# Linear attention and a channel mix on one Trainium2 core: q of batch 4's first group turned by the DMA crossbar, with a new order of all instructions

## The chip, the cores and the metric

The kernel runs on one core of one Trainium2 chip. The metric is the device time of one execution in microseconds, lower is better. Times of several runs are given by their median; one further execution was taken with the hardware profiler, and all rows below are from it.

## The reference

Eight batches, eight heads, 576 positions, head width 64. The output of the attention goes, with the heads side by side (512 channels), into a channel mix.

```
def _attn_ref(q, k, v):                       # (8, 8, 576, 64) each
    q_s = exp(q - max(q, -1)); q_s = q_s / sum(q_s, -1)
    k_s = exp(k - max(k,  2)); k_s = k_s / sum(k_s,  2)
    kv = einsum('bhsd,bhse->bhde', k_s, v)
    return einsum('bhsd,bhde->bhse', q_s, kv)

def _moe_ref(x, mu_k, mu_r, w_k, w_v, w_r):   # x (8, 576, 512), w_k to 1024 and w_v back
    x_prev = x shifted by one position, zero first
    xk = mu_k * x + (1 - mu_k) * x_prev
    xr = mu_r * x + (1 - mu_r) * x_prev
    v = max(xk @ w_k, 0) ** 2 @ w_v
    return v / (1 + exp(-(xr @ w_r)))
```

## The kernel before, in words

**Groups.** The attention is done in 16 groups (b, g): batch b, and of it four heads, two on each half of the partitions and two beside each other (`load`, L190). For each group q, k and v are loaded as f32; ACT takes the exponentials of q and k (`exp`, L326) and casts v (`cast_v`, L332); DVE sums q's exponentials, takes reciprocals and scales q (`rsum`, `rrec`, `scale_q`, L341 to L353). TensorE (PE) forms K-V products and the sums of k (`kv`, L389), and for batch 0 the sums apart (`zs`, L380).

**Turning q.** The product of q with K-V needs q with its width on the partitions. There are two ways. In the first, PE transposes the scaled q, 64 rows at a time, against an identity into PSUM (`transpose_q`, L362: 18 or 36 matmuls) and ACT copies the result to the tile qt (`copy_qt`, L371). In the second, for the groups in the tuple CROSSBAR (L40), SP issues a DMA that transposes from the tile qs to the tile qt (L516), and neither PE nor ACT has a part in it. Such a DMA makes 1,152 packets of 256 bytes in the trace.

**Blocks.** From batch 2 on, PE's work for a group is one block, named B with batch and group (L447): the X product of the group before it, which the list `pending` holds over (`x`, L532); the transposes of q, unless the crossbar does them; and K-V. B40 is the block of (4, 0) and holds X of (3, 1); B41 holds X of (4, 0). The first groups have T (transposes), KV and Z (sums) or, in batch 1, a TKV block, and X products of their own, in which the mix's weights are already folded (`mixed_x`, L480). After X, ACT and DVE copy, shift and mix x into the rings xk and xr.

**Units.** The mix works through ten units of up to 512 positions. In a name such as k37, r21, v230, the first digit is the unit: k is a block of 128 columns of the product with w_k (`k_part`, L618, four matmuls; in units 0 and 1 the first four blocks come in two parts), r one with w_r (`r_part`, L650, four), v one with half of w_v (`v_part`, L670, four). Units 4 and 9 have 256 positions. ACT applies ReLU and tanh, DVE squares and gates, and SP stores in halves of 128 KB from the seven th buffers (L682).

**The order.** Nothing is scheduled by a tool. The string ORDER (L43) lists every operation by name, and for those that take buffers their numbers after a colon; each engine gets its instructions in this order. Within one engine, a waiting instruction holds all behind it. POOL issues nearly all loads (eleven raw buffers), and each of its DMAs waits for the landing of the one eight places before it. SP issues the first loads, all stores and the crossbar's transposes. `fill` (L292) are matmuls of zeros at the start that write a bank of PSUM.

Of the kernel before, what the change touches and what calls it, by code (L numbers as in the profile page):

```python
# [51 lines left out]
X001:0.3 kvn01:1 wp010:1 k02:0 x0010 edge01 k00:1 x0011 X010:1.0 load11q1 k03:2 x0100 x0101 k01:3
wv0 rsum100:2 k00.2 expk100:2 load10v1:7 k02.2 wp011 expq110:0 k03.2 relu00:0 k01.2 load10v0
X011:0.1 relu01:1 k07:1 sq01:0 load11v0:8 sq00 expq101 k05:3 load11v1 relu02:2 rsum101 relu03:1
k06:0 rrec100 sq02 relu05:0 sq03 x0110 k04:2 x0111 relu06:2 sq05 load11k1:9 r00:3 relu07:1
load11k0 expk101 r02:0 expq111 wv1 r03:1 relu04:0 rsum111:3 th00:0 r01:2 sq07 th03:1 sq04 rrec101
th02:2 scale101:2 v020:3 wv2 scale100 cast101:0 v030:1 load20v0:10 rrec111 cast100 scale111:0
muload v000:0 th01:3 rsum110 cast110:1 v010:2 load20q0:0 rrec110 cast111 scale110 TKV10:0
expk111:0 load21q0:2 expk110 load30q0:1 rz10:2 kvn10:0 TKV11:1 qt10:2 wp100:0 load20k0:3 v011
load21v0:4 rz11:0 sq06 v031 kvn11:1 edge10 qt11:0 v021 wp110:1 load61v0:6 v001 v032 edge11 v002  # L60
cast200:2 X100:0.1 load21k0:5 o00 v022 load31q0:7 x1001 x1000 v012 o02 expq200:1 wp111 mu:0
X110:1.0 mucopy k13:3 load30v0:8 x1101 x1100 k11:0 wp101 o01 expq210:2 k13.2 rsum200:0 k11.2
load31k0:9 relu13:1 X111:0.1 relu11:0 load40q0:10 k12:2 x1111 x1110 k17:3 o03 expk200:1 load30k0:0
sq11:1 k10:0 st03.2 sq13 k16:1 st00 expq300:0 rrec200 rsum210:1 load40v0:2 st03 X101:1.0 st01
relu17:2 k12.2 x1011 st00.2 x1010 k10.2 load31v0:3 sq17 relu16:0 k14:3 scale200:1 relu10:1
relu12:2 r12:1 cast210:0 sq10 load60q0:1 TKV20:0 rsum300:2 relu14:1 r11:0 th12:4 rrec210 rrec300
load41q0:4 rz20:1 expk210:2 k15:2 sq12 w20:0 scale210:2 r10:3 qt20:1 v120:1 sq16 relu15:2
scale300:0 expq310:1 B21:1.0 load50q0:5 sq14 th10:5 v110:2 rz21:2 sq15 xs20:0 xb20 w21:1
load40k0:7 rsum310:3 v100:3 qt21:0 v121 edge20 diff20:0 th11:6 v111 cast300:1 sc2000:0 X21:0.1
sc2011:1 o11 r13:0 xs21:1 load41k0:8 xb21 sc2010 o12 v101 expk300:0 edge21 rrec310 r20:2 diff21:1  # L70
expk310:1 load41v0:0 sc2001 v130:1 sc2101:2 mix200 th20:1 load60v0:9 TKV30:1 sc2100 th13:0
sc2111:0 mix210 v131 cast310:2 sc2110 k27:2 cast400:0 o13 load51q0:3 rz30:0 k21:0 scale310:1
st13.2 relu27:0 load50k0:2 st13 expq400:2 k22:1 o10 k20:2 w30:2 relu22:1 load71v0:10 st10 mix201
qt30:2 st11 k23:3 sq27:0 st11.2 rsum400:0 relu21:2 k24:1 st01.2 relu23:0 st10.2 B31:0.1 mix211
expk400:2 sq23 k26:0 rz31:1 relu24:0 rrec400 load50v0:7 sq21 xb30:0 w31:0 k25:3 sq24 scale400:2
relu20:2 r22:1 xs30 qt31:1 sq20 r23:2 edge30 diff30:0 relu25:0 B40:1.0 relu26:2 sq22 sc3001:2
expq410:0 v200:3 sc3000 mix300 th22:0 v220:0 load71k0:4 rz40:2 sq25 th23:6 rsum410:1 xs31:1 r21:1
xb31 v230:2 sq26 expq500:1 edge31 sc3011:1 v201 diff31:1 cast410:1 load61q0:5 w40:1 v231 sc3101:0
sc3100 th21:3 rrec410 load61k0:0 mix310 v221 expq510:2 o23 r30:1 o20 qt40:0 load71q0:3 k33:2
scale410:0 st20.2 th30:5 st20 k37:3 relu33:1 st12.2 o22 k40:1 st12 relu37:0 sc3111:2 v210:2 sc3010  # L80
st02 expk410:0 rsum500:2 st02.2 k41:0 k35:3 expq600:0 load51k0:8 mix301 v211 sc3110 relu40:2
load51v0:1 sq37:1 k32:1 relu35:0 o21 expk500:1 sq33 B41:0.1 mix311 relu41:1 load70q0:2 sq35 k31:3
rz41:0 sq40:0 relu32:0 w41:2 sq41 k30:2 sq32 relu31:2 rsum510:3 cast500:2 k34:0 r31:1 relu30:1
rsum600:0 load70v0:7 relu34:0 r33:3 th31:1 sq30 xs40:0 rrec510 k36:2 xb40 rrec500 sq31 sq34 k44:0
scale500:1 relu36:1 r32:1 relu44:2 k43:2 edge40 qt50:1 th32:4 diff40:0 v330:0 qt41:2 sq36 v310:1
rrec600 st23.2 sc4001:0 th33:2 scale510:2 v331 expq610:1 k46:3 sc4000 qt51:0 relu43:0 o33
load60k0:5 B50:1.0 relu46:1 cast510:0 scale600:0 k47:2 st23 k42:0 cast600:1 v300:3 load70k0:1 sq46
qt60:2 sq44 rz50:1 mix400 v311 relu47:1 xs41:1 xb41 v320:2 o31 relu42:2 sq47 v301 expq700:2 st31.2
edge41 sq42 diff41:1 st21 r41:1 st21.2 expk510:2 o30 v321 sc4101:1 st30.2 sc4100 sq43 st31 k45:0
sc4110:2 mix410 st30 r40:3 relu45:1 expk600:0 o32 v410:0 sq45 rsum610:1 th41:6 k50:2 sc4111 k52:1  # L90
relu50:2 w50:0 rsum700:2 cast610:2 v411 k51:2 relu52:0 o41 mix411 k53:1 relu51:1 rrec610 B51:0.1
sq51:1 sq50 k54:0 scale610:1 xb50:1 v400:2 relu53:1 sc4010:0 relu54:2 rz51:2 sq52 k55:1 expq710:0
sc4011 rrec700 mix401 v401 relu55:0 rsum710:3 k56:0 th40:3 expk610:1 k57:1 sq53 sq54 relu56:1 sq55
r50:3 w51:1 relu57:2 scale700:2 r51:0 th50:1 cast700:0 v500:1 rrec710 o40 sq56 v510:3 th51:5 st40
sq57 xs50 st41 edge50 B60:1.0 st33 diff50:1 v501 st32.2 xb51:0 sc5000:1 st41.2 rz60:0 sc5001 v511
xs51 st40.2 w60:2 expk700:2 mix500 qt61:1 r52:2 o50 expk710:0 o51 B61:0.1 st50 edge51 v520:0
st50.2 sc5010:2 diff51:0 th52:6 st22 r53:1 cast710:1 st51 sc5011 sc5100:0 st51.2 sc5101 v521
sc5110:1 th53:3 mix510 v530:3 sc5111 rz61:1 mix511 k60:2 o52 xb60:0 v531 w61:0 st52 mix501
relu60:0 st32 k61:1 scale710:0 xs60 st52.2 B70:1.0 st22.2 relu61:1 o53 k62:0 xb61:1 sq60:0 st53
edge60 k63:2 relu62:2 st53.2 diff60:1 xs61 st33.2 k64:1 sq61 relu63:0 qt70:0 sc6000:0 sc6001 k65:3  # L100
sc6010:1 relu64:1 mix600 k66:0 sq62 edge61 relu65:2 sq63 k67:2 diff61:0 relu66:0 r60:1 sq64
sc6100:2 relu67:1 sc6101 r61:3 sq65 th60:1 mix610 v600:0 sq66 th61:5 sc6011 sq67 v610:2 sc6110:0
sc6111 mix601 v601 mix611 v611 rz70:2 w70:1 r62:1 o60 o61 st60 r63:3 th62:4 st60.2 v620:0 st61
th63:6 st61.2 v630:2 v621 v631 o62 k70:1 st62 o63 st62.2 k71:3 relu70:2 st63 st63.2 k72:0 sq70:1
relu71:0 qt71:2 k73:2 sq71 relu72:1 k74:1 sq72 relu73:2 k75:3 sq73 relu74:0 k76:0 sq74 relu75:1
k77:2 sq75 relu76:2 r70:1 sq76 relu77:0 B71:0.1 sq77 th70:0 v700:3 xb70:0 rz71:0 w71:2 r71:0 v701
th71:3 xs70 v710:2 o70 edge70 X71:1.0 st70 diff70:1 v711 xb71:1 st70.2 sc7000:2 r72:1 sc7001 xs71
o71 r73:0 edge71 st71 th72:2 mix700 st71.2 v720:3 diff71:0 th73:1 sc7010:1 v730:2 sc7100:0 sc7101
sc7110:2 v721 mix710 sc7111 v731 sc7011 o72 k80:1 mix711 st72 k81:0 st72.2 o73 relu80:1 mix701
st73 k82:3 relu81:2 st73.2 sq80:0 k83:2 sq81 relu82:0 k84:1 sq82 relu83:1 k85:0 sq83 relu84:2  # L110
k86:3 sq84 relu85:0 k87:2 sq85 relu86:1 r80:1 sq86 relu87:2 r81:0 sq87 th80:5 v800:3 th81:4 v810:2
v801 v811 o80 r82:1 st80 o81 st80.2 r83:0 th82:6 st81 st81.2 v820:3 th83:0 v830:2 v821 v831 o82
k90:1 st82 o83 k91:0 st82.2 relu90:0 k92:3 st83 relu91:1 sq90:1 k93:2 relu92:2 sq91 st83.2 k94:1
relu93:0 sq92 k95:0 relu94:1 sq93 k96:3 relu95:2 sq94 k97:2 relu96:0 sq95 r90:1 relu97:1 sq96 sq97
r91:0 th90:3 v900:3 th91:2 v901 v910:2 o90 v911 st90.2 st90 v910.2:1 o91 v911.2 st91.2 st91 o91.2
# [722 lines left out]
```

## Time and profile before

| | before |
|---|---|
| runs, median of 3 (lowest to highest) | 196.73 us (196.01 to 197.06) |
| profiled execution, its own time | 196.33 us |
| its span | 194.6 us |
| busy: PE, DVE, ACT, POOL | 186.5, 150.0, 140.7, 43.5 us |
| TensorE's granted clock, mean | 0.997 |
| DMA | 41.86 MB, mean 215 GB/s |

The span runs from the first to the last instruction of the program; the execution's own time has some 1.8 us around it. Rows of a timeline give start, length, engine, line, operation, out<-in with sizes, and in square brackets the idle time of that engine ahead of it and what ended it. Line numbers are those of the kernel before; in the changed kernel every line behind ORDER is one lower. A matmul of 128x512 starts 0.216 us after the one before it when PE is dense; its row is longer since matmuls are pipelined.

### The profile page before, as it was taken

The numbers are of one execution on the slowest core, as the hardware profiler recorded it, in microseconds if no ns is written. First come the engines' busy times: TensorE is split into PE (matmuls) and PEld (weight loads), VectorE is DVE, ScalarE is ACT, GpSimd is POOL, SyncE is SP. The second block draws the span as 40 slices with busy tenths as digits, with TensorE's granted clock in tenths as the row PEclk, the third lists the DMA queues.
The fourth block names the chain that finished last, engine by engine and source line by source line (L and its number), as shares of the span: only waits on it lengthen the run. The fifth ranks groups of instructions, "written<-read, shape, count | busy, mean of one in ns | idle before, by whom it ended". The sixth has DMA issues, their size and how long they took to land.

```text
span 194.6 us, 4767 instructions
## 1 busy us (share of the span) xinstructions
PE 186.5 (96%) x1873; PEld 90.6 (47%) x1873; DVE 150.0 (77%) x347; ACT 140.7 (72%) x218; POOL 43.5 (22%) x70
## 2 busy tenths in 40 slices
PE   7789999999999999999999999999999999999991
PEld 2254445445444554554555444444444444444751
DVE  1788658799999999999989998999924469622531
ACT  3678799899999999989996798767225742752440
POOL 8444348694324212341110000000000000000000
PEclk9999999999999999999999999999999999999998
DMA  6999999999999999899699604887049122404413
GB/s 200 316 261 291 267 351 302 397 394 393 414 390 394 394 407 334 280 333 320 171 212 125 220 0 100 172 190 154 0 110 138 34 54 54 111 0 95 94 29 108
DMA packets 23646, 41.86 MB, mean 215 GB/s; under 512 B 9404, under 2 KB 12744, under 8 KB 23624
## 3 DMA queue, kind: packets, MB, share of 16 engines
...
q14 instruction: 8, 0.07, 0.1%
HBM read 33.56 MB, written 9.44 MB: 221 GB/s over the span
## 4 chain that ended last, share of the span: by engine, by line
PE 81%; DMA 12%; POOL 3%; ACT 2%; issue 0%; DVE 0%; POOLq 0%
PE mm_c L672 11%; PE mm_d L672 9%; PE mm_c L620 8%; PE mm_a L620 7%; PE mm_b L620 7%; DMA wk_bb<-in_moe_w_k_dram 7%; PE mm_b L652 7%; PE mm_d L620 7%; PE mm_a L672 6%; DMA raw_h<-in_v_dram 5%; PE mm_b L672 5%; PE mm_a L652 4%; PE mm_d L652 3%; PE mm_c L652 1%; PE att_b L396 1%; PE att_a L536 1%
## 5 line engine op out<-in xcount | busy, mean ns | idle before, releaser
L672 PEld LDWEIGHTS <-k_a 128*128 128x128 bf16 x144 | 13.8, 98 | 16.4 <-issue 0.2
L652 PEld LDWEIGHTS <-xr 128*128 128x128 bf16 x144 | 13.9, 98 | 16.1 <-issue 0.2
L672 PEld LDWEIGHTS <-k_b 128*128 128x128 bf16 x152 | 14.4, 98 | 15.0 <-issue 0.2
L652 PE MATMUL mm_b<-wr,xr 128*128 128x512 bf16 x64 | 16.4, 379 | 0.0
L620 PEld LDWEIGHTS <-wk_ab 128*128 128x128 bf16 x80 | 7.6, 98 | 8.2 <-issue 0.8
L620 PEld LDWEIGHTS <-wk_bb 128*128 128x128 bf16 x80 | 7.8, 98 | 7.7
L620 PEld LDWEIGHTS <-wk_aa 128*128 128x128 bf16 x80 | 7.4, 98 | 8.2 <-issue 0.9
L620 PEld LDWEIGHTS <-wk_ba 128*128 128x128 bf16 x80 | 7.5, 98 | 7.8 <-issue 0.2
L652 PE MATMUL mm_a<-wr,xr 128*128 128x512 bf16 x36 | 9.3, 380 | 0.0
L672 PE MATMUL mm_c<-wv_a,k_a 128*128 128x512 bf16 x32 | 8.2, 379 | 0.0
L607 ACT ACTIVATE rel_b<-mm_b 128x512 bf16<-128x512 f32 (+1 forms) x7 | 4.0, 570 | 4.9 <-PE mm_b L620 4.8
L607 ACT ACTIVATE rel_a<-mm_b 128x512 bf16<-128x512 f32 (+1 forms) x8 | 4.6, 573 | 4.0 <-PE mm_b L620 3.6
L620 PE MATMUL mm_c<-xk,wk_aa 128*128 128x512 bf16 (+1 forms) x26 | 7.3, 363 | 0.0
L620 PE MATMUL mm_c<-xk,wk_ab 128*128 128x512 bf16 (+1 forms) x26 | 7.3, 363 | 0.0
L611 DVE TENSOR_TENSOR k_a<-rel_b 128x512 bf16<-128x512 bf16 (+1 forms) x14 | 5.4, 383 | 2.5 <-ACT rel_b L607 2.5
L672 PE MATMUL mm_d<-wv_a,k_b 128*128 128x512 bf16 x28 | 7.2, 379 | 0.0
L652 PE MATMUL mm_d<-wr,xr 128*128 128x512 bf16 x28 | 7.2, 379 | 0.0
L611 DVE TENSOR_TENSOR k_b<-rel_a 128x512 bf16<-128x512 bf16 (+1 forms) x14 | 5.5, 391 | 1.8 <-ACT rel_a L607 1.3
L607 ACT ACTIVATE rel_c<-mm_a 128x512 bf16<-128x512 f32 (+1 forms) x11 | 6.0, 550 | 0.7 <-PE mm_a L620 0.7
L611 DVE TENSOR_TENSOR k_b<-rel_b 128x512 bf16<-128x512 bf16 (+1 forms) x14 | 5.5, 391 | 1.3 <-ACT rel_b L607 0.9
L611 DVE TENSOR_TENSOR k_b<-rel_c 128x512 bf16<-128x512 bf16 (+1 forms) x12 | 4.7, 392 | 1.9 <-ACT rel_c L607 1.6
L620 PE MATMUL mm_d<-xk,wk_ba 128*128 128x512 bf16 (+1 forms) x22 | 6.1, 360 | 0.0
...
## 6 DMA issues: line engine op xcount, KB each, us to landing
...
```

What stands on the lines that cost most here:

```text
L396: kn.nc.tensor.matmul(kn.half(slot, r)[two[u], KVO:KVO + n], lhsT=kn.eks[ek.index][two[r], j, u, :], rhs=by, start=(j == 0), stop=(j == J ...
L536: kn.nc.tensor.matmul(kn.half(slot, u)[two[r], to:to + n], lhsT=kn.ws[w.index][two[u], r, :], rhs=x_columns(r, u, at, n), start=True, stop ...
L607: kn.nc.scalar.activation(out=kn.rels[rel.index][:, 0:n], in_=kn.bank(kf)[:, 0:n], func=ACT.Relu, scale=HALF_ROOT)
L611: kn.nc.vector.tensor_tensor(out=kn.k2s[k2.index][:, fc, 0:n], in0=kn.rels[rel.index][:, 0:n], in1=kn.rels[rel.index][:, 0:n], op=ALU.mult)
L620: kn.nc.tensor.matmul(kn.bank(kf)[:, 0:n], lhsT=kn.wk[fc // 4][ct % 2][:, ct // 2, (fc % 4) * 128: (fc % 4) * 128 + 128], rhs=kn.xs[0][:, ...
L652: kn.nc.tensor.matmul(kn.bank(rps), lhsT=kn.xs[1][:, ct, c:c + 128], rhs=kn.wr[:, ct, :], start=(ct == 0), stop=(ct == CT - 1))
L672: kn.nc.tensor.matmul(kn.bank(vps)[:, 0:width], lhsT=kn.k2s[k2.index][:, ft, 128 * m:128 * m + 128], rhs=wv_of(ft)[:, part], start=(ft == ...
```

## The change

The tuple of the groups whose q the crossbar turns gets a seventh member, (4, 0). Its 36 transposes and ACT's copy are gone with it, and SP issues a transposing DMA for it (qt40). ORDER is replaced as a whole: the same operations, permuted, with other buffer numbers. Cut to what the text speaks of:

```diff
-CROSSBAR = tuple((b, g) for b in range(5, B) for g in range(2))
+CROSSBAR = ((4, 0),) + tuple((b, g) for b in range(5, B) for g in range(2))
...
 ORDER = """
...
-load00k1 load01v late load01k0:3 load10q0:4 wk00 wk01 expq001:0 expq000 load11q0:5 rsum001:0
...
+load00k1 load10q0:3 load01k0:4 load01v wk00 load10q1 expq001:0 expq000 wk10 rsum001:0 rsum000 wk01
+expk000:0 rrec001 ACT!load01k1 wk11 rrec000 scale001:0 expq011:1 fill:1 fill.2:2 fill.3:3 fill.4:0
...
-widecopy wk10 rrec010 fill.17:1 KV001:0 rrec011 scale010:1 KV000 fill.18:2 fill.19:3 T00:1 rest
-Z00 qt00:0 scale011 rz00:0 expk010:1 fill.20:1 fill.21:1 T01:3 edge00 kvn00:0 load10q1 expk011
-fill.22:1 KV010:2 wp000:0 expq100:2 wr wp001 X000:1.0 qt01:1 KV011 x0001 Z01 load10k1 x0000 rz01:1
+rrec010 fill.17:1 fill.18:2 KV001:0 scale010:1 KV000 T00:1 rest Z00 qt00:0 rz00:0 scale011
+load11q0 expk010:1 kvn00:0 fill.19:3 fill.20:1 fill.21:1 T01:3 edge00 wp000:0 expk011 wp001
+X000:2.1 expq100:2 load10k0:6 qt01:1 fill.22:2 KV010:0 x0001 KV011 Z01 wr x0000 X001:1.3 rz01:1
...
+relu21:0 st12.2 B31:1.0 relu22:1 mix201 relu23:2 sq22 k24:3 cast400:0 rz31:1 rrec400 w31:0 mix211
+k26:0 relu20:1 load70v0:3 sq21 xs30:0 scale400:2 xb30 r22:1 r23:2 relu24:0 edge30 qt40:0 sq20
+qt31:1 sq24 k25:3 diff30:0 th22:4 B40:0.1 sq23 relu26:1 sc3001:0 r21:1 sc3000 relu25:0 rz40:2
...
```

In the order built from it, PE has 36 transposes fewer, ACT one copy fewer and SP one transposing DMA more; POOL's loads are the same set in another order. In the first stretch POOL now queues q of (1, 0) ahead of v of (0, 1), and w_k's tile wk10 ahead of wk01. On ACT the first half of k of (0, 0) goes ahead of q of (0, 1). On PE the transposes T00 follow KV000 directly, and the last zero matmul, fill.22, writes the third of the mm banks, one of the two that the transposes of (0, 1) have filled.

More of the change, by code (lines that the diff above doesn't have):

```diff
@@ L44 @@
 ACT!load00q0:0 zero ident load00q1 ACT!load00k0:1 load01q1:2 ACT!load01q0 rows load00v consts warm
-load00k1 load01v late load01k0:3 load10q0:4 wk00 wk01 expq001:0 expq000 load11q0:5 rsum001:0
-ACT!load01k1 rsum000 load10k0:6 expq011:1 rrec001 wk11 rrec000 rsum011:1 fill:1 fill.2:2 fill.3:3
-fill.4:0 fill.5:1 fill.6:2 fill.7:3 fill.8:0 fill.9:1 fill.10:2 fill.11:3 fill.12:0 fill.13:1
-fill.14:2 fill.15:3 fill.16:0 wide:0 scale000:0 expq010 expk000:0 rsum010 expk001 scale001
-widecopy wk10 rrec010 fill.17:1 KV001:0 rrec011 scale010:1 KV000 fill.18:2 fill.19:3 T00:1 rest
@@ L50 @@
-Z00 qt00:0 scale011 rz00:0 expk010:1 fill.20:1 fill.21:1 T01:3 edge00 kvn00:0 load10q1 expk011
-fill.22:1 KV010:2 wp000:0 expq100:2 wr wp001 X000:1.0 qt01:1 KV011 x0001 Z01 load10k1 x0000 rz01:1
[L52 to L115, printed above, removed]
@@ L116 @@
-st91.4 st91.3
+load00k1 load10q0:3 load01k0:4 load01v wk00 load10q1 expq001:0 expq000 wk10 rsum001:0 rsum000 wk01
+expk000:0 rrec001 ACT!load01k1 wk11 rrec000 scale001:0 expq011:1 fill:1 fill.2:2 fill.3:3 fill.4:0
+fill.5:1 fill.6:2 fill.7:3 fill.8:0 fill.9:1 fill.10:2 fill.11:3 fill.12:0 fill.13:1 fill.14:2
+fill.15:3 fill.16:0 wide:0 scale000 expq010 rsum011:1 rsum010 expk001 rrec011 widecopy load11q1:5
+rrec010 fill.17:1 fill.18:2 KV001:0 scale010:1 KV000 T00:1 rest Z00 qt00:0 rz00:0 scale011
@@ new lines @@
+load11q0 expk010:1 kvn00:0 fill.19:3 fill.20:1 fill.21:1 T01:3 edge00 wp000:0 expk011 wp001
+X000:2.1 expq100:2 load10k0:6 qt01:1 fill.22:2 KV010:0 x0001 KV011 Z01 wr x0000 X001:1.3 rz01:1
+kvn01:1 edge01 k02:0 wp010:1 x0010 k00:1 x0011 load10k1 X010:0.1 k03:2 x0100 x0101 k01:3 wv0
+expq101 wp011 rsum101:2 k02.2 load10v0:7 k00.2 relu02:0 rrec101 rsum100 k03.2 relu00:1 X011:0.1
+load10v1 relu03:2 sq00:0 k01.2 x0110 load11v1:8 sq03 k07:0 relu01:1 load11v0 expq111:0 k06:1 sq01
+load11k1:9 x0111 expq110 k05:2 scale101:2 relu07:2 rrec100 k04:3 sq07 relu05:1 sq02 relu06:2
@@ new lines @@
+rsum111:3 r03:0 load11k0 expk100:2 rsum110 relu04:0 r01:2 wv1 rrec111 late th03:0 r02:1 expk101
+rrec110 scale100 th01:1 r00:3 th02:2 scale110:0 v020:0 wv2 scale111 th00:3 load20v0:10 sq06 v000:2
+cast101:0 muload v030:1 cast100 cast111:1 TKV10:0 load20q0:0 cast110 v010:3 rz10:2 expk111:0
+load21q0:2 kvn10:0 sq05 expk110 load30q0:1 sq04 qt10:2 TKV11:1 v031 rz11:0 kvn11:1 v011 wp100:0
+qt11:0 wp111:1 v001 edge10 wp110 v021 wp101 v002 X100:0.1 cast200:2 o00 load20k0:4 v012 edge11
+load21k0:3 x1001 v022 x1000 v032 o01 load21v0:5 expq200:1 X110:1.0 o02 load31q0:6 mu:2 x1101 k13:3
@@ new lines @@
+x1100 load30v0:7 k11:0 o03 expq210:2 X111:0.1 load40q0:8 rsum200:0 st03.2 k13.2 x1110 load31k0:9
+st01.2 k17:1 relu13:2 st00 load31v0:10 x1111 expq300:0 st02 k11.2 mucopy rsum210:1 st00.2 k12:3
+load30k0:0 X101:0.1 st01 relu11:1 relu17:0 k10:2 rrec200 sq11:1 load40k0:2 x1010 k12.2 sq17 k15:0
+sq13 expk200:1 x1011 k14:1 scale200:1 relu15:1 relu12:0 k10.2 relu14:2 k16:0 rrec210 sq12
+expk210:2 load51q0:1 sq15 r12:3 rsum300:2 relu10:0 TKV20:0 cast210:0 load41v0:4 r10:1 rz20:1
+rrec300 w20:0 relu16:1 sq14 r11:2 sq10 qt20:1 scale210:2 v120:0 th10:4 load40v0:3 expq310:1 sq16
@@ new lines @@
+B21:1.0 scale300:0 th12:5 r20:1 load50q0:5 xb20:0 rz21:2 rsum310:3 v110:3 xs20 th11:6 load60q0:6
+v121 w21:1 edge20 qt21:0 diff20:0 v100:2 cast300:1 sc2000:0 rrec310 X21:0.1 sc2001 v111 o12 xb21:1
+load41q0:7 sc2011:1 mix200 r13:0 xs21 th20:3 edge21 v101 o11 expk300:0 diff21:1 v130:1 expk310:1
+sc2010 load41k0:0 sc2110:2 TKV30:0 sc2101:0 sc2100 expk400:2 load50v0:9 v131 mix210 o10 th13:1
+load50k0:2 k27:3 cast310:2 rz30:0 scale310:1 st10 k20:2 st11 relu27:2 st10.2 load60v0:10 sc2111
+k22:0 expq400:2 st03 sq27:0 w30:2 st12 o13 k21:3 qt30:2 load71q0:8 rsum400:0 st13 k23:1 st13.2
@@ new lines @@
+relu21:0 st12.2 B31:1.0 relu22:1 mix201 relu23:2 sq22 k24:3 cast400:0 rz31:1 rrec400 w31:0 mix211
+k26:0 relu20:1 load70v0:3 sq21 xs30:0 scale400:2 xb30 r22:1 r23:2 relu24:0 edge30 qt40:0 sq20
+qt31:1 sq24 k25:3 diff30:0 th22:4 B40:0.1 sq23 relu26:1 sc3001:0 r21:1 sc3000 relu25:0 rz40:2
+w40:1 xs31:1 expq410:0 sq26 r30:0 sq25 sc3011:1 v230:3 th21:0 rsum410:1 load51v0:7 th30:1 v220:1
+xb31 mix300 v200:0 expq500:1 edge31 rrec410 diff31:1 v221 th23:5 load51k0:5 sc3100:2 v231
+expq510:2 sc3101 mix310 v201 cast410:1 o22 load61q0:1 k37:2 o20 load61v0:4 scale410:0 k41:1 st20.2
@@ new lines @@
+relu37:2 k32:0 relu41:1 cast500:2 sc3010 v210:2 o23 relu32:0 sq37:1 k40:1 load70q0:9 st23 sc3111:0
+v211 mix301 relu40:2 expk410:0 k33:3 sq40:0 o21 load60k0:0 k43:0 rsum500:2 relu33:2 st21.2 k31:1
+expk500:1 st20 st02.2 B41:0.1 sq32 sc3110 st23.2 relu31:0 load71v0:2 sq33 k35:2 st21 rrec500
+xs40:0 mix311 xb40 st11.2 sq31 k30:3 relu35:2 rz41:0 sq41 edge40 expq600:0 rsum510:3 r31:1 k34:2
+relu43:0 load61k0:6 th31:3 sq35 rsum600:0 k44:0 relu30:1 k36:1 relu34:2 sq34 k46:3 rrec600
+relu36:2 w41:2 r32:2 sq30 scale500:1 relu44:1 r33:1 th32:2 qt41:2 k47:0 sq43 qt50:1 sq36 v330:2
@@ new lines @@
+diff40:0 th33:5 rrec510 B50:1.0 relu47:0 sq44 relu46:2 scale510:2 v320:1 xs41:1 xb41 v331 sc4000:2
+expq610:1 edge41 scale600:0 v310:0 cast510:0 load70k0:1 v300:3 o33 cast600:1 sc4001 load71k0:7
+v311 diff41:1 k42:2 o31 v301 relu42:1 sc4101:1 cast610:2 st31.2 mix400 k45:0 st31 r41:2 sq42
+qt51:0 sc4100 expk510:2 o30 v321 rz50:1 mix410 relu45:1 st30.2 expk600:0 v410:3 sq46 st30 sc4110:0
+sq47 qt60:2 sc4011:2 k51:0 sq45 sc4111 o32 v411 relu51:2 rsum610:1 expq700:2 k50:1 w50:0 k52:0
+th41:0 mix411 relu50:0 k53:2 sq51:1 rsum700:2 B51:0.1 relu53:1 r40:1 xb50:1 sc4010 o41 k54:2 sq50
@@ new lines @@
+relu52:2 rrec610 sq52 v400:3 relu54:0 rrec700 rz51:2 scale610:1 expq710:0 k55:0 v401 mix401
+relu55:2 th40:6 sq54 k56:2 rsum710:3 expk610:1 k57:0 relu56:0 sq53 r50:1 w51:1 relu57:1 scale700:2
+r51:2 th50:3 cast700:0 sq55 v500:0 rrec710 o40 v510:1 th51:1 sq56 st40 sq57 xs50 st41 edge50
+B60:1.0 diff50:1 st33 v501 xs51:0 st40.2 xb51 sc5000:1 st41.2 rz60:0 sc5001 r52:3 w60:2 cast710:1
+mix500 v511 o50 expk700:2 v520:2 st50 o51 st50.2 expk710:0 edge51 B61:0.1 sc5010:0 qt61:1 diff51:0
+r53:0 th52:6 sc5011 sc5100:2 v521 st51 sc5101 th53:0 sc5110:1 st51.2 mix510 v530:1 st32.2 sc5111
@@ new lines @@
+st22 rz61:1 mix511 k60:3 o52 xb60:0 v531 st52 k62:0 xs60 st32 relu60:2 o53 st52.2 w61:0 k61:2
+mix501 st22.2 st53 scale710:0 B70:1.0 st33.2 k66:3 xb61:1 st53.2 edge60 qt70:0 sq60:0 k65:1
+relu61:0 diff60:1 relu62:1 k63:2 sc6001:2 sq61 sc6000 k64:0 sq62 relu63:2 sc6010:1 xs61 mix600
+r62:2 relu64:0 edge61 relu65:1 sq63 k67:0 diff61:0 relu66:2 r60:1 sq64 relu67:0 r61:3 th60:3 sq67
+sc6100:0 r63:0 sc6101 th61:1 sq66 th62:2 sq65 v600:1 mix610 th63:6 sc6011 v610:3 sc6110:2 mix601
+v601 sc6111 rz70:2 mix611 v620:2 o60 v611 w70:1 st60 k70:0 o61 v621 relu70:0 k71:1 o62 v630:3
@@ new lines @@
+st62.2 relu71:2 st60.2 k73:0 st61.2 v631 k72:2 o63 sq70:1 k74:1 st63 relu72:1 sq71 st63.2 relu73:0
+k75:3 sq72 qt71:2 relu74:2 sq73 k76:2 sq74 relu75:1 k77:0 sq75 relu76:0 r70:1 sq76 relu77:2
+B71:0.1 sq77 th70:4 v700:3 xb70:0 rz71:0 w71:2 r71:2 v701 th71:5 xs70 v710:0 o70 edge70 X71:1.0
+st70 diff70:1 v711 xb71:1 st61 st62 sc7000:0 r72:1 sc7001 xs71 st70.2 o71 r73:2 edge71 st71 th72:0
+mix700 st71.2 v720:3 diff71:0 th73:3 sc7010:1 v730:0 sc7100:2 sc7101 sc7110:0 v721 mix710 sc7111
+v731 sc7011 o72 k80:1 mix711 st72 k81:2 st72.2 o73 relu80:1 mix701 st73 k82:3 relu81:0 st73.2
@@ new lines @@
+sq80:0 k83:0 sq81 relu82:2 k84:1 sq82 relu83:1 k85:2 sq83 relu84:0 k86:3 sq84 relu85:2 k87:0 sq85
+relu86:1 r80:1 sq86 relu87:0 r81:2 sq87 th80:6 v800:3 th81:1 v810:0 v801 v811 o80 r82:1 st80 o81
+st80.2 r83:2 th82:2 st81 st81.2 v820:3 th83:4 v830:0 v821 v831 o82 k90:1 st82 o83 k91:2 st82.2
+relu90:2 k92:3 st83 relu91:1 sq90:1 k93:0 relu92:0 sq91 st83.2 k94:1 relu93:2 sq92 k95:2 relu94:1
+sq93 k96:3 relu95:0 sq94 k97:0 relu96:2 sq95 r90:1 relu97:1 sq96 sq97 r91:2 th90:5 v900:3 th91:0
+v901 v910:0 o90 v911 st90.2 st90 v910.2:1 o91 v911.2 st91.2 st91 o91.2 st91.4 st91.3
```

## The prediction

> **What bounds the kernel now.** I read the chain of work that ended last, then the stretches before and after 33.7 us, then TensorE's (PE's) own waits.
>
> ```profile
> PE 81%; DMA 12%; POOL 3%; ACT 2%; issue 0%; DVE 0%; POOLq 0%
> ```
>
> ```profile
> 16.20:33.70 17.50, 17.16 (x205) 8.09 (x205) 12.39 (x32) 15.01 (x28) 9.40 (x16) 1.00 1.15 296
> 33.70:190.50 156.80, 156.79 (x1475) 76.38 (x1469) 127.22 (x277) 115.55 (x176) 24.97 (x37) 1.00 0.67 203
> ```
>
> The columns are the length of the stretch, then busy time of PE, weight loads, DVE, ACT and POOL, the granted clock, the DMA share and GB/s. From 33.7 to 190.5 us PE is busy 156.79 of 156.80 us at clock 1.00, and the list of PE's waits for that stretch is empty. There only two things move the end: less PE work, or a wait that PE does not have today. Before 33.7 the loads decide. The last wait is this one, in the timeline of PE:
>
> ```profile
> 32.62 0.44 PE L366 MATMUL att_b<-ident,qs_a 64*128 64x64 bf16 x18
> 33.26 0.48 PE L396 MATMUL att_b<-vv_b,ek_a 64*64 64x65 bf16 x36 [0.21 <-ACT ek_a L327]
> 33.68 0.60 PE L672 MATMUL mm_c<-wv_b,k_a 128*128 128x512 bf16 x2
> ```
>
> Group (1,1)'s K-V products wait 0.21 us for the exponential of its k (raw_j), which lands at 31.8 and 32.5 us in the trace and goes through ACT at 31.85 to 33.20.
>
> **The transposes of (4,0).** Compare a block that transposes on PE with one that the crossbar serves, both in PE's timeline:
>
> ```profile
> 85.11 0.59 PE L620 MATMUL mm_b<-xk,wk_ab 128*128 128x512 bf16 x2
> 85.64 0.22 PE L536 MATMUL att_a<-qt_a,w_b 64*64 64x64 bf16 x4
> 85.69 0.39 PE L536 MATMUL att_b<-qt_a,w_b 64*64 64x512 bf16 x4
> 85.91 0.48 PE L366 MATMUL att_a<-ident,qs_a 64*64 64x64 bf16 x36
> 86.21 0.49 PE L396 MATMUL att_a<-vv_b,ek_a 64*64 64x65 bf16 x36
> 86.63 0.60 PE L620 MATMUL mm_d<-xk,wk_aa 128*128 128x512 bf16 x2
> ```
>
> ```profile
> 109.47 0.59 PE L620 MATMUL mm_b<-xk,wk_ab 128*128 128x512 bf16 x2
> 110.00 0.22 PE L536 MATMUL att_a<-qt_b,w_a 64*64 64x64 bf16 x4
> 110.05 0.39 PE L536 MATMUL att_b<-qt_b,w_a 64*64 64x512 bf16 x4
> 110.27 0.48 PE L396 MATMUL att_a<-vv_a,ek_c 64*64 64x65 bf16 x36
> 110.68 0.60 PE L620 MATMUL mm_a<-xk,wk_ba 128*128 128x512 bf16 x2
> ```
>
> From the same two matmuls ahead to the matmul behind: 86.63 - 85.11 = 1.52 us against 110.68 - 109.47 = 1.21 us. The 36 transposes cost **0.31 us** of PE, on the path. Block B40 (71.59 to 72.58 us) loses exactly these. ACT loses one copy of qT, 1.00 us from start to next start (79.32 to 80.32 us). PE waits for nothing there, so I cost it at nothing; a copy more would only matter if ACT, busy 4.00 of 4.00 us in 66 to 70, became late.
>
> **What it adds.** One crossbar transpose on SP's queue. After DVE's scaling of q (it ends at 70.73 us now and stands at the same place among its neighbours), SP issues it at about 70.9 us, taking 1.3 to 1.5 us as the six do now. Its reader is the X product inside block B41. Between B40 and B41 the changed order puts 14 groups of four 512-column matmuls (0.864 us each, as the row r at 69.77 to 70.63 shows) and 3 of four 256-column ones (0.44, the half): 12.1 + 1.3 = 13.4 us. Block B40 starts at 71.5 as now (the PE work from TKV11 to B40 is 37.56 us in both orders) and takes 1.09 - 0.31 = 0.78 us, so B41 is due at 71.5 + 0.78 + 13.4 = **85.7 us**. The transpose has 14.8 us. How long it takes is the open price. The trace has both ends:
>
> ```profile
> DMA to landing us min/median/max: 3.3/3.3/3.3
> ...
> DMA to landing us min/median/max: 4.4/8.2/11.9
> ```
>
> These are qt_a's (issued at 133.4) and qt_c's (148.5 and 98.5). The 11.9 is the one at 98.5 us, the only one that a load ran into:
>
> ```profile
> 70.00:74.00 4.00, 4.00 (x95) 2.12 (x94) 3.93 (x11) 3.92 (x7) 0.27 (x1) 1.00 1.04 406
> 101.00:105.00 4.00, 4.00 (x22) 2.01 (x21) 4.00 (x12) 2.94 (x4) 0.00 (x0) 1.00 1.32 205
> ```
>
> With the transpose and a load in flight together the engines moved 205 GB/s, against 406 at 70 to 74 us, where the new one goes. There it also queues behind stores of SP that are still going out: th_g's stores land 2.2 us after issue at the least and 8.2 here, 6.0 us longer. So the bounds are 3.3 + 6.0 = 9.3 us (landing at 80.2, no wait, 5.5 us early) and 11.9 + 6.0 = 17.9 us (landing at 88.8, 3.1 us late). I take the lower for the forecast, since five of the six are nearer to it (two land after 3.3 and 4.4 us, and the packets of the other three, issued at 93.24, 96.16 and 122.76, end 2.7 to 2.8 us after issue), and keep 3.1 us for the range. SP's stores behind it start at st20, over 8 us later, so no buffer waits at the lower price.
>
> The Trainium skill (DMA: Bandwidth & Descriptors, "Issuing engines are not separate DMA queues") says that DMAs from all issuers run on the same 16 engines and interleave. The trace agrees for stores: from 70 to 74 us it has 62 load packets and 58 store packets a microsecond, nearly one for one. If that holds for the transpose's 1,152 packets (72 an engine, 0.02 us each, beside load packets of 0.18), it would take 72 x 0.20 = 14.4 us and land about 3 us late; the sum would then be that of the second rival. The page Advanced Engine Details and Errata ("X-Bar Transpose (TRN2)") says that these DMAs are as fast as regular ones; by that nothing is late.
>
> **The start.** Two zero matmuls (10.75 and 10.97 us) go from ahead of T00, and ACT takes the k exponentials earlier (ek_a now ends at 10.10 because it stands behind the late raw_c; its first half moves ahead, so about 9.5). T00 moves from 11.28 to about 10.2, and the qT copy from 11.76 to 10.7. But then ACT runs the same five steps as before (copy, two of ek_b, eq_c, qt_b: 1.02 + 0.58 + 0.58 + 0.57 + 1.05), and in the new order a zero matmul into mm_c stands ahead of KV010 on PE and must wait until qt_b's first half is copied out: 10.7 + 2.75 + 0.65 = 14.1. Behind it queue 0.22 of itself, 0.7 for the K-V products, 0.35 for their sums and 0.7 for X001 with 0.2 of changes between them: first w_k matmul at about 16.3, where it is now (16.27). Bounds: 1.0 us earlier if that wait is shorter, 0.9 later if the copy must end whole. Nor would a gain reach the end: the loads that POOL queues up to raw_j are the same set in another order, so raw_j still lands near 32.5 and the row at 33.26 stays, for which at most 0.21 us is to be had. Weights wr (23.9 now) move behind 288 KB more, about 0.8 us at 355 GB/s (the rate from 28.3 to 39.0 us), and are needed at 24.8: just in time. I take **0**.
>
> **The rest of the order.** PE's list holds the same groups, permuted; no group is added. With no waits now, a permutation can only lose; I take 0, and up to 0.5.
>
> **Sum.** -0.31 + 0 + 0 = -0.3 us: span 194.6 to 194.3, the profiled execution 196.33 to 196.0. The median of the runs, 196.73, lies 0.40 above that execution; **196.4 us**.
>
> **Rivals.**
> 1. *The late transpose* (slower). Price above: at 17.9 us B41 waits 3.1, PE stands, and everything behind shifts: 196.73 - 0.31 + 3.1 = 199.5. It decides once the transpose takes over 14.8 us. For it: the row at 101, the 406 GB/s at 70 to 74. Against: five of six took far less, though none of these with loads beside it.
> 2. *The same, and loads fall behind.* At half rate for 12 us, loads lose some 6 us; then (5,0)'s transpose, which today is issued at 93.24 just as the loads pause, meets the backlog, and the loss repeats: -0.31 + 2 x 3.1 = +5.9, 202.6.
> 3. *The start pays.* raw_j lands earlier too: -1.0 - 0.31, 195.4. Against: the same bytes ahead of it.
> 4. *The start loses* 0.9: 197.3.
> That the change does not do what it says is excluded by the built order: seven transposes on SP, 36 fewer on PE, no zero matmul next to T00.
>
> **Chances.** Forecast 0.43, rival 1 0.27, rival 2 0.17, rival 3 0.07, rival 4 0.06. Half a per cent (0.98 us) is about what a measurement of this kernel can tell from no change. Faster: 0.07 and 0.02 from the forecast's edge = 0.09. Within: 0.41 + 0.06 = 0.47. Slower: 0.27 + 0.17 = 0.44. The forecast's own range is 195.7 to 197.1 (0.5 from permutation above, noise of the runs below). The range must reach rival 1 with some of rival 2: 195.7 to 201.0, which leaves out most of rivals 2 and 3, about 0.2.
>
> **What would show it.** Right: PE's waits after 33.7 stay empty, the new qt_a transpose lands by 85, the block with X of (3,1) is 0.78 us long, K-V of (1,1) starts at 33.2. Wrong: a wait before B41's X matmuls (L535) on a DMA from qs_c, GB/s near 200 in 74 to 86 us, or loads after 86 us landing late; for rival 3, raw_j landing before 31.5.

## The result, and the profile after

The changed kernel takes **198.72 us** (median of 22 runs, 197.70 to 203.06); the kernel before, on the same chip, 197.12 us (22 runs, 195.95 to 198.40). The ratio is **1.0095** (95% interval 1.007 to 1.012): slower, by about 1.9 us. Ratios here are formed over undisturbed runs only, so they are not quite the quotients of the medians. The profiled execution took 199.09 us, its span is 197.3 us (before: 194.6).

The chain of work that ended last has changed its make-up. PE had 81% of it, now:

```profile
PE 59%; ACT 14%; DMA 12%; DVE 9%; issue 3%; ACTq 1%; SPq 0%; DVEq 0%
```

PE's list of waits, empty after 33.7 us before, now has two rows of over 0.2 us there (columns: total us, times, longest):

```profile
PE mm_b L619 <- ACT th_d L656: 1.9, 1, 1.9
...
PE mm_a L671 <- ACT th_b L656: 0.7, 1, 0.7
```

Both wait for a tanh on ACT that still holds the PSUM bank. ACT's timeline shows what the two tanh wait for in their turn:

```profile
76.19 0.60 ACT L656 ACTIVATE th_b<-mm_a 128x512 f32<-128x512 f32 x1 [1.16 <-DMA out_dram<-th_b]
```

```profile
93.13 0.60 ACT L656 ACTIVATE th_d<-mm_b 128x512 f32<-128x512 f32 x1 [2.00 <-DMA out_dram<-th_d]
```

It is not the reader of the new transpose. It is the buffer that the tanh writes: an earlier tile of th_b (th_d) has not yet landed in DRAM. The pieces of the chain, in order of time, give how long each store took from issue to landing:

```profile
66.83 9.25 DMA out_dram<-th_b
...
86.05 6.98 DMA out_dram<-th_d
```

and SP's timeline where the second one stood:

```profile
81.20 0.48 SPq L687 DMA_DIRECT2D out_dram<-th_d  x1
83.34 0.47 SPq L687 DMA_DIRECT2D out_dram<-th_f  x1
85.53 0.47 SPq L687 DMA_DIRECT2D out_dram<-th_a  x1
86.05 0.59 SPq L687 DMA_DIRECT2D out_dram<-th_d  x1
```

The two halves of one tile of th_d are issued 4.85 us apart, though both were ready at 81.2. Between them stand two stores that wait for DVE to gate other tiles. In the kernel before, the same tile (th20, there in th_b) had its halves stored together (SP's timeline, the two as one row), and the tanh that next writes its buffer (th31 in both orders) waited for nothing (ACT's timeline):

```profile
79.47 1.11 SPq L688 DMA_DIRECT2D out_dram<-th_b  x2
```

```profile
90.29 0.60 ACT L657 ACTIVATE th_b<-mm_b 128x512 f32<-128x512 f32 x1
```

One other tanh of before already waited for its buffer, without any wait of PE:

```profile
74.13 0.60 ACT L657 ACTIVATE th_g<-mm_c 128x512 f32<-128x512 f32 x1 [0.21 <-DMA out_dram<-th_g]
```

The rest answers to the rows of before. The block of (4, 0), with the two matmuls ahead and the matmul behind:

```profile
71.29 0.59 PE L619 MATMUL mm_d<-xk,wk_bb 128*128 128x512 bf16 x2
71.81 0.22 PE L535 MATMUL att_a<-qt_b,w_a 64*64 64x64 bf16 x4
71.86 0.39 PE L535 MATMUL att_b<-qt_b,w_a 64*64 64x512 bf16 x4
72.08 0.48 PE L395 MATMUL att_a<-vv_a,ek_c 64*64 64x65 bf16 x36
72.50 1.04 PE L651 MATMUL mm_b<-wr,xr 128*128 128x512 bf16 x3
```

72.50 - 71.29 = 1.21 us, as forecast. K-V of (1, 1) starts at 33.20 (33.26 before). The new transpose stands in SP's timeline here; its issue alone takes 4.28 us, not the 1.3 to 1.5 of the six others before:

```profile
70.44 4.28 SPq L515 DMA_TRANSPOSE qt_a<-qs_c  x1
```

And the stretches (length, busy PE, weight loads, DVE, ACT, POOL, clock, DMA share, GB/s) show the transpose among loads:

```profile
74.00:78.00 4.00, 3.29 (x16) 1.45 (x15) 2.65 (x6) 2.84 (x5) 0.72 (x1) 1.00 1.08 292
78.00:82.00 4.00, 4.00 (x22) 1.97 (x21) 3.93 (x7) 3.98 (x6) 1.81 (x3) 1.00 1.33 74
```

74 GB/s, with a DMA share of 1.33: the packets take more than all the time of the 16 engines and move almost nothing. Of those that start there, 612 are the transpose's, of 256 bytes, and 30 are of loads. This is the row that misleads, as the experiments show. The span's +2.7 us are -0.31 (transposes) + 0.7 + 1.9 (the two waits) and 0.4 in pieces of 0.2 and less.

### The profile page after: what moved, and what is told of

Its sections match the earlier page's. It is cut to its first block, busy times and chain, and to the rows that moved or that the text cites. A ratio compares the mean times of both kernels' runs of the same rounds, so it can differ in the third digit from the quotient of the medians.

```text
span 197.3 us, 4661 instructions
## 1 busy us (share of the span) xinstructions
PE 185.5 (94%) x1812; PEld 90.2 (46%) x1837; DVE 150.1 (76%) x345; ACT 138.9 (70%) x218; POOL 43.7 (22%) x70
## 4 chain that ended last, share of the span: by engine, by line
PE 59%; ACT 14%; DMA 12%; DVE 9%; issue 3%; ACTq 1%; SPq 0%; DVEq 0%
PE mm_d L671 9%; PE mm_a L619 7%; PE mm_a L671 6%; PE mm_c L619 5%; DMA out_dram<-th_b 5%; PE mm_b L619 4%; PE mm_b L651 4%; PE mm_b L671 4%; PE mm_c L651 4%; PE mm_d L619 4%; DMA out_dram<-th_d 4%; DMA raw_c<-in_q_dram 3%; PE mm_c L671 3%; PE mm_a L651 1%; PE att_a L395 1%
## 5 line engine op out<-in xcount | busy, mean ns | idle before, releaser
L671 PEld LDWEIGHTS <-k_a 128*128 128x128 bf16 x144 | 13.8, 98 | 17.3 <-issue 1.2
L671 PEld LDWEIGHTS <-k_b 128*128 128x128 bf16 x152 | 14.4, 98 | 15.2 <-issue 0.5
L651 PE MATMUL mm_c<-wr,xr 128*128 128x512 bf16 x48 | 12.3, 379 | 0.1
L606 ACT ACTIVATE rel_a<-mm_a 128x512 bf16<-128x512 f32 (+1 forms) x9 | 5.0, 553 | 5.7 <-PE mm_a L619 5.4
L671 PE MATMUL mm_d<-wv_a,k_a 128*128 128x512 bf16 x31 | 8.0, 379 | 0.2 <-issue 0.2
L606 ACT ACTIVATE rel_c<-mm_b 128x512 bf16<-128x512 f32 (+1 forms) x8 | 4.5, 564 | 5.2 <-PE mm_b L619 4.4
L619 PE MATMUL mm_a<-xk,wk_ba 128*128 128x512 bf16 (+1 forms) x28 | 7.5, 349 | 0.0
L619 PE MATMUL mm_a<-xk,wk_bb 128*128 128x512 bf16 (+1 forms) x27 | 7.3, 347 | 0.0
L619 PE MATMUL mm_a<-xk,wk_ab 128*128 128x512 bf16 (+1 forms) x24 | 6.7, 361 | 0.1
L610 DVE TENSOR_TENSOR k_a<-rel_a 128x512 bf16<-128x512 bf16 (+1 forms) x13 | 5.2, 399 | 1.8 <-ACT rel_a L606 1.8
L619 PE MATMUL mm_a<-xk,wk_aa 128*128 128x512 bf16 (+1 forms) x23 | 6.5, 361 | 0.0
L606 ACT ACTIVATE rel_b<-mm_a 128x512 bf16<-128x512 f32 (+1 forms) x11 | 6.3, 574 | 0.3 <-PE mm_a L619 0.2
```

Of the source, the lines that this page charges most:

```text
L606: kn.nc.scalar.activation(out=kn.rels[rel.index][:, 0:n], in_=kn.bank(kf)[:, 0:n], func=ACT.Relu, scale=HALF_ROOT)
L610: kn.nc.vector.tensor_tensor(out=kn.k2s[k2.index][:, fc, 0:n], in0=kn.rels[rel.index][:, 0:n], in1=kn.rels[rel.index][:, 0:n], op=ALU.mult)
L619: kn.nc.tensor.matmul(kn.bank(kf)[:, 0:n], lhsT=kn.wk[fc // 4][ct % 2][:, ct // 2, (fc % 4) * 128: (fc % 4) * 128 + 128], rhs=kn.xs[0][:, ...
L651: kn.nc.tensor.matmul(kn.bank(rps), lhsT=kn.xs[1][:, ct, c:c + 128], rhs=kn.wr[:, ct, :], start=(ct == 0), stop=(ct == CT - 1))
L671: kn.nc.tensor.matmul(kn.bank(vps)[:, 0:width], lhsT=kn.k2s[k2.index][:, ft, 128 * m:128 * m + 128], rhs=wv_of(ft)[:, part], start=(ft == ...
```

## The experiments

**Theory A**, my first: the crossbar transpose collides with loads and stores from 75 to 82 us, and so the stores land late. **Theory B**: the new order gives the two tanh buffers whose stores are issued too late, and the transpose only stands beside. Theories C and D, about loads, are named where they come up. E1 and E2 take the change apart.

**E1, the order without the new transpose.**

```diff
-CROSSBAR = ((4, 0),) + tuple((b, g) for b in range(5, B) for g in range(2))
+CROSSBAR = tuple((b, g) for b in range(5, B) for g in range(2))
...
-edge30 qt40:0 sq20
+edge30 sq20
...
-cast410:1 o22
+cast410:1 qt40:0 o22
```

> The changed order, but q of (4,0) is turned by PE and ACT again; the six other crossbar transposes stay. Theory A (the crossbar transpose runs into loads and stores from 75 to 82 us, and so the stores that free th_b and th_d land late): both new waits of PE (0.7 us for the tanh into th_b near 76, 1.9 us for the one into th_d near 93) shrink to 0.3 us or less, PE gets its 0.31 us of transposes back, the DMA rate from 78 to 82 us stays above 250 GB/s instead of 74: ratio to the kernel before 0.997 to 1.004. Rival B (the new order itself gives th buffers to tanh whose stores are issued too late; the transpose only stands beside): both waits stay, 0.31 is added: 1.009 to 1.013.

Measured: 1.0111 (1.0075 to 1.0147). **Theory A fell** as the cause of the loss. Without the seventh transpose the kernel is as slow, and both waits are there:

```profile
PE mm_b L619 <- ACT th_d L656: 1.1, 1, 1.1
PE mm_a L671 <- ACT th_b L656: 0.7, 1, 0.7
```

The wait on th_d is 0.8 us shorter in this one execution. Of that, 0.3 us is PE's, which comes to the wait at 92.23 instead of 91.92 us. The other 0.5 us is the store's: it lands at 92.57 instead of 93.03, 6.3 us after issue instead of 7.0. So that store was 0.7 us slower with the transpose, in one execution of each, which is a small part of what A claims. What comes back in place of the transpose is PE's 0.31 us and 0.3 us for a ReLU near 82.7 us, which ACT's copy of q (81.02 to 82.03) now holds up; the runs' times do not resolve the rest. The GB/s from 78 to 82 us fell here too, to 144, with a DMA share of 0.49 instead of 1.33: with less to do, not with a jam.

**E2, the new transpose without the order.** CROSSBAR as in the changed kernel, in the order of before `qt40:0` moves from behind `o20` to behind `scale400:2`.

> The order of before, with the one edit that q of (4,0) is turned by the crossbar, issued behind its scaling at about 70.7 us. Theory A: the transpose meets loads in flight until 79 us, takes 8 to 12 us, and the loads issued at 77 and 78 us and the stores of 79.5 to 82 fall 3 to 5 us behind; some buffer is then waited for, 0.5 to 3 us: ratio 1.001 to 1.014. Rival B: only PE's 0.31 us goes: 0.998 to 0.999, and PE's list of waits after 33.7 us stays empty.

Measured: 0.999 (0.996 to 1.002). No row in PE's list of waits after 33.7 us. B's number, 0.998 to 0.999, is the one met: the crossbar's part costs nothing that can be seen, and its gain of 0.31 us (0.0016) is under what these runs resolve.

**E4, the transpose out of the loads' way.**

```diff
-load50k0:2 k27:3 ... st10.2 load60v0:10 ... load71q0:8 ... load70v0:3 ... load51v0:7 ... load51k0:5
+load50k0:2 k27:3 ... st10.2 ... load51v0:7 ... load51k0:5 load60v0:10 load71q0:8 load70v0:3
```

> The changed kernel, with the loads of v of (6,0), q of (7,1) and v of (7,0), which are in flight when the transpose starts, put two places later in POOL's queue (behind v and k of (5,1)), so that no load lands between about 73 and 80 us. Theory A: the transpose lands by 77 us (12.0 us after issue now, 7 or less then), the th_b wait falls to 0.2 or less and the th_d wait goes: ratio to before 0.995 to 1.001. Rival B: the waits stay, for the stores are in the same places of SP's queue: 1.007 to 1.011. If the postponed loads come too late for batches 6 and 7, new waits after 100 us show it.

Measured: 1.0078 (1.0048 to 1.0109). The transpose was issued at 71.85 and landed at 76.72 us, 4.9 us, so the collision was gone, and with it the wait on th_b. That wait was not the transpose's, for E1 has it without the transpose: what E4 moved away from the store into DRAM is the loads. The wait on th_d stayed:

```profile
PE mm_b L619 <- ACT th_d L656: 1.7, 1, 1.7
```

A's numbers are met on the transpose and on th_b, B's on the time. (In the profiled executions of E4 and E6 TensorE's clock was 0.50 from 12 to 18 us, and their first w_k matmul came 1.0 to 1.3 us later than the changed kernel's. Their spans are therefore no measure; the ratios do not rest on these two executions alone.)

**E3, other buffers.** The stores `st02.2` and `st11.2` go behind `st02` and `st11`, and from `th30` on numbers 1 and 2, 3 and 6 change places:

```diff
-th30:1 ... th31:3 ... th32:2 ... th40:6
+th30:2 ... th31:6 ... th32:1 ... th40:3
```

> The changed kernel with its crossbar transpose. Two stores that were left for late in SP's queue (second halves of th_c and th_g) are issued with their first halves, 20 to 45 us earlier, and from th30 on the buffers th_b and th_c, th_d and th_g change places, so that the two tanh that wait now find a buffer free. Theories A and B alike: both waits of PE vanish, the transpose still takes about 12 us: 2.6 us less than the changed kernel, ratio to before 0.995 to 1.000. Rival C (the loads that the transpose holds up cost as much by themselves, and the stores only hide it): PE waits for an exponential or cast fed by a late load instead, ratio above 1.004.

Measured: 1.0004 (0.9975 to 1.0033), span 194.4 us, no wait of PE over 0.2 us after 33.7. As far as the runs resolve it, the whole loss was in those two buffers. It is 1.8 us in the runs, not 2.6; the intervals allow that. The loads that the transpose held up cost nothing, so C falls. The transpose itself ran among the loads here as well (the row is of the writes of qt_a, from issue):

```profile
DMA to landing us min/median/max: 4.4/5.3/13.8
```

The 13.8 is the new one, issued at 70.01, landed at 83.86.

**E5, one store moved.**

```diff
-st20.2
+st20.2 st20
...
-expk500:1 st20 st02.2 B41:0.1
+expk500:1 st02.2 B41:0.1
```

> The changed kernel with one store moved: the second half of the first tile of unit 2 (st20, from th_d) goes right behind its first half in SP's queue, ahead of st23 and st21.2, for whose gating it waits there today (issued at 86.05 us, 4.85 us after the first half, landed at 93.03, when the tanh into th_d had waited 2.00 us). Theory B (two stores stand too late in the new order, and the crossbar transpose is innocent): it is issued near 81.8 and lands by 90, PE's wait of 1.9 us on that tanh goes to 0, the 0.7 us on th_b stays: ratio to before 1.000 (0.997 to 1.003). Rival D (the backlog of loads behind the transpose makes every store of that time take 7 to 9 us, so that another tanh waits in its place): 1.005 to 1.010.

Measured: **1.0005** (0.9973 to 1.0037), span 194.4. The two halves are one row of SP again, and the tanh into th_d has no wait in brackets:

```profile
80.33 1.12 SPq L687 DMA_DIRECT2D out_dram<-th_d  x2
```

```profile
89.99 0.62 ACT L656 ACTIVATE th_d<-mm_b 128x512 f32<-128x512 f32 x1
```

One position of one store brings back what the change lost, as far as the runs resolve, with the crossbar transpose in place (PE still waits 0.5 us on th_b). B holds. D is right that the stores are slow there (this half landed 7.8 us after issue), but no other tanh waits in its place.

**E6, the first wait alone.** `st02.2` goes behind `st02`, and only numbers 1 and 2 change places from `th30` on.

> The changed kernel with only the first of the two waits taken away: the second half of th_c is stored with its first half near 42 us instead of at 86, and from th30 on th_b and th_c change places, so that th30 finds a free buffer. Theory B: PE's wait of 0.7 us near 76 goes, the one on th_d stays 1.7 to 2.0, because st20 hangs behind the same gating, which comes earlier by the same 0.7: ratio to before 1.004 to 1.008. Rival D: the th_d wait grows to 2.6, for its store lands when the backlog lets it: 1.008 to 1.011.

Measured: 1.006 (1.0024 to 1.0096). PE's wait on th_b is gone, that on th_d is 2.0. As B expects; the two parts, 0.9% (E5) and 0.35%, do not quite add to E3, within their intervals.

**E12, the same store later.**

```diff
-expk500:1 st20 st02.2 B41:0.1 sq32 sc3110 st23.2
+expk500:1 st02.2 B41:0.1 sq32 sc3110 st23.2 st20
```

> The changed kernel with st20 two places later in SP's queue, behind st02.2 and st23.2: the dose the other way. Theory B: it is issued 1.2 to 1.3 us later (near 87.3), lands as much later, and PE's wait on the tanh into th_d grows from 1.9 to about 3.1: ratio to before 1.013 to 1.019 (the changed kernel 1.0095). Rival (that wait is really for something else that ends at the same time, a load or an exponential ahead on ACT): 1.007 to 1.012.

Measured: **1.030** (1.0238 to 1.0363), 203.55 us. The direction is B's, the size is twice what I expected: the store was issued at 87.17, 1.1 us later, its tanh started 7.8 us after that, against 7.1 in the changed kernel, and so the wait was 3.8 us, not 3.1. And then PE itself was slow (stretches of 2 us):

```profile
PE mm_b L619 <- ACT th_d L656: 3.8, 1, 3.8
```

```profile
92.00:94.00 2.00, 0.00 (x0) 0.00 (x0) 0.03 (x1) 0.00 (x0) 0.00 (x0) 1.00 1.03 409
94.00:96.00 2.00, 0.34 (x1) 0.10 (x1) 0.00 (x0) 0.99 (x3) 0.00 (x0) 0.56 1.04 416
96.00:98.00 2.00, 2.00 (x8) 0.92 (x7) 1.38 (x5) 1.02 (x3) 0.00 (x0) 0.50 0.71 281
98.00:100.00 2.00, 2.00 (x7) 0.81 (x6) 2.00 (x4) 0.43 (x2) 0.00 (x0) 0.50 0.08 29
100.00:102.00 2.00, 2.00 (x11) 0.91 (x10) 2.00 (x5) 1.88 (x3) 0.00 (x0) 0.73 0.78 148
```

The granted clock falls to 0.50 while PE idles and comes back at 101.1. PE works again from 95.66, so it does 5.4 us of work at half speed and loses 2.7 by it: 3.8 - 1.9 + 2.7 = 4.6 us over the changed kernel. The spans of the two profiled executions differ by 4.5 us (201.8 and 197.3), the ratios by 2.05%, 4.0 us.

**E8, the crossbar's part in the mended order.** E3 with E1's edit.

> The kernel with the exchanged th buffers (1.0004), but q of (4,0) turned by PE and ACT again: the crossbar's part alone, in the new order with its two store waits gone. Theory B with the forecast's own term: PE gets 0.31 us back and nothing else changes, 0.0016 above that kernel, 1.000 to 1.004, and no wait of PE over 0.3 us after 34 us. Rival D (the transpose costs by the loads it holds up, which the freed buffers did not show): this kernel is faster than that one by over 0.5 us, below 0.998.

Measured: 1.0027 (0.9994 to 1.006), against E3's 1.0004: 0.0023 apart, 0.0016 forecast. The sign is as forecast; the intervals do not tell it from zero. Here too a ReLU stands behind ACT's copy:

```profile
81.67 1.02 PE L671 MATMUL mm_c<-wv_a,k_a 128*128 128x512 bf16 x4 [0.49 <-ACT rel_c L606]
```

The prediction took the copy that goes from ACT at nothing. In the order of before that holds, in this one the copy, where I put it, costs PE 0.3 to 0.5 us.

**E7 and E11, the start.** E7 is E3 without the token `fill.22:2`. E11 is the kernel before with two zero matmuls moved:

```diff
-widecopy wk10 rrec010 fill.17:1 KV001:0 rrec011 scale010:1 KV000 fill.18:2 fill.19:3 T00:1 rest
-Z00 qt00:0 scale011 rz00:0 expk010:1 fill.20:1
+widecopy wk10 rrec010 fill.17:1 fill.18:2 KV001:0 rrec011 scale010:1 KV000 T00:1 rest
+Z00 qt00:0 scale011 rz00:0 expk010:1 fill.19:3 fill.20:1
```

> The kernel with the exchanged th buffers (ratio 1.0004, span 194.4 us) without the last zero matmul, which waits 0.9 us there for ACT's copy of q's transposes and holds the K-V products of (0,1) behind it. If the start is bound by loads, as the prediction held: the first w_k matmul comes earlier than 16.29 us, by up to 0.9, but K-V of (1,1) stays at 33.1 and the span at 194.4 +- 0.2; ratio within 0.002 of the other's. Rival: the gain reaches the end, K-V of (1,1) comes before 32.7 us: span 193.9 or less.

Measured: 0.9977 (0.9945 to 1.001). First w_k matmul at 15.20 instead of 16.29, K-V of (1, 1) at 32.52 instead of 33.12:

```profile
32.52 0.48 PE L395 MATMUL att_b<-vv_b,ek_a 64*64 64x65 bf16 x36
```

The first number holds in every profile: 15.20 to 15.25 in the three kernels without that zero matmul (E7, E9, E10), 15.79 and more in all others. The second does not, for single executions spread as widely: E8, whose start is that of E3, has K-V of (1, 1) at 32.62, and E9, whose start is that of E7, at 33.45. In E3, E5 and E8 it starts 16.83 us after the first w_k matmul, so there PE's own work sets it and not a load. The span is 195.1, and K-V of (2, 0) starts at 48.46 against 48.26: in the profiled execution the next waits (0.6 us for a copy to xk among them) take it all. The ratio lies 0.0027 (0.5 us) under E3's, where I expected 0.002 at most; the intervals do not resolve it.

> The kernel before with the third named part of the change alone: the two zero matmuls ahead of T00 go elsewhere (one ahead of the first K-V products, one behind the sums Z00). T00 starts at 10.8 or before instead of 11.28 us and ACT copies it as much earlier; the loads still set the row at 33.26, so by the prediction's start term the time stays: 0.998 to 1.002. Rival (the start pays in full): 0.997 or less.

Measured: 0.9989 (0.9956 to 1.0022): the two moved zero matmuls alone make no difference that can be told. Its profiled execution does not show the parts well: the first K-V products came at 10.86 us (10.15 before), behind a later exponential, and T00 at 11.45 instead of 10.8 or before.

**E9, an eighth group.** E7, `st20` as in E5, and q of (4, 1) by the crossbar too:

```diff
-CROSSBAR = ((4, 0),) + tuple((b, g) for b in range(5, B) for g in range(2))
+CROSSBAR = ((4, 0), (4, 1)) + tuple((b, g) for b in range(5, B) for g in range(2))
...
-st20.2
+st20.2 st20 qt41:2
```

> The kernel with the exchanged th buffers, without the last zero matmul, with st20 right behind st20.2, and with q of (4,1) turned by the crossbar as well (eight groups; its transpose stands behind st20 in SP's queue, near 82 us, and its reader's block comes near 98). Theory B (a transpose among loads costs only if somebody waits): another 0.31 us of PE goes and nothing is waited for, span 193.9 to 194.2, ratio to before 0.996 to 0.999. Rival D: two transposes hold up some 10 us of loads, casts and exponentials of batches 5 and 6 come late, and PE waits 1 to 3 us near 95 to 112 us: 1.004 to 1.014.

Measured: 1.0307 (1.0249 to 1.0365). B failed here, and D's account is only partly right: no load is waited for, the transpose itself is.

```profile
PE att_b L535 <- DMA qt_c<-qs_a: 4.6, 1, 4.6
```

It was issued at 81.86 us and its reader started at 99.82: 18 us. The first transpose landed only at 85.31, 0.8 us before its own reader (86.15). Then the loads that had been held up went beside the second one: from 91 to 98 us 624 packets of transposes and 525 of loads started. The wait again brought the clock to 0.50, for 6.8 us.

**E10, all mended.** E7 with `st20` as in E5.

> Exchanged th buffers, no last zero matmul, and st20 right behind st20.2. From the kernel with the first two (0.9977): the store had slack there already, so nothing more is gained: 0.995 to 1.000, no wait of PE over 0.3 us after 40 us. A version for both kernels to be held against.

Measured: 0.998 (0.9945 to 1.0014), no wait of PE over 0.3 us after 40 us. It beats the changed kernel; from the kernel before it can't be told.

## Why the prediction was wrong, point by point

1. **Transposes gone, -0.31 us: right.** The block is 1.21 us long, and E2 and E8 agree in size, within what they resolve.
2. **The crossbar's transpose: right in effect, wrong in size.** Nothing waited for it. Among loads it landed 9.8 (E10), 9.9 (E7), 13.85 (E3) and 15.0 us (E9) after issue, and in the changed kernel its last packet ended 12.4 us after issue: inside the bounds of 9.3 and 17.9, mostly above the 9.3 that I took. Its reader came later than the 14.8 us that I gave it (15.85 us after issue in E3), so even 15.0 was in time. The estimate of 14.4 us came from a page of the Trainium skill (DMA: Bandwidth & Descriptors, "Issuing engines are not separate DMA queues": DMAs of all issuers share 16 engines and interleave). E3's 13.85 is near it by luck: 5.75 us of it passed before the first packet started, and beside the 1,152 packets then only 131 of loads started, not one for one. E9's second transpose comes nearer to that, and E4's 4.9 shows the case with the loads moved away. The prediction also misread its own estimate: 14.4 us is less than the 14.8 it had, so the transpose would have landed 0.4 us early and not 3 late, and a single wait is the first rival's sum, not the second's. The Trainium skill's page Advanced Engine Details and Errata ("X-Bar Transpose (TRN2)") says that such DMAs are as fast as regular ones; the row with 74 GB/s beside 1.33 of DMA share does not agree, where loads are in flight. Rival 1's mechanism (B41 waits for the transpose) is real, and E9 shows it, one transpose later.
3. **The start, 0: right** by the row of K-V of (1, 1) (33.20) and by E11. The reason, that the loads stand at that row whatever comes ahead, was too strong: in E3, E5 and E8 PE's own work set it (E7 above).
4. **"The rest of the order. PE's list holds the same groups, permuted; no group is added. With no waits now, a permutation can only lose; I take 0, and up to 0.5": this step failed.** It lost 2.6 us in the profile and 2.2 in the runs (1.9 and the 0.31 that was gained; E1's 1.0111, the order alone, is 2.2 too). I looked at PE's list and not at the list that the buffers hang on. The evidence was in the order's text: before, `st20.2 th30:5 st20`; after, `st20.2`, then `st23`, `st21.2`, and only then `st20`. In the trace of before, the second half of th20's tile went at about 80.0 (the row at 79.47 is both) and the next tanh into that buffer ran at 90.29, 10.3 us later. In the changed kernel the last half went at 86.05 and ACT stood ready for that tanh at 91.13, 5.1 us later, with stores taking 7. And the prediction had the price on the page: a store of th_g, issued at 65.84 us, took 8.2 us to land. In the trace of before a tanh even waited 0.21 us for that store (the row at 74.13 above), so the buffer had no slack left there.
5. **"SP's stores behind it start at st20, over 8 us later, so no buffer waits at the lower price": wrong,** though not by the transpose. The first to wait was a buffer whose stores stood ahead of it (th_b: 9.25 us to land, against 8.2 from issue to where ACT stood ready, 75.03), the second one behind a store that waits for DVE.
6. **The chances.** The time, 198.7, lies in the range and near rival 1's 199.5, but by luck: what made it is in none of the rivals. A rival "a th buffer comes free late", with the stores' issue and landing against the next tanh, should have stood in place of rival 2.

Still open: why the transpose's time among loads spreads from 9.8 to 15.0 us, and whether the 0.5 us of E7 and E10 are real. The reordered loads and exponentials of the start were never run apart from the rest of the order; E3 has them in, and its time can't be told from that of the kernel before.
